# Infini-attention with a token MLP on one core: which of two query blocks comes first in the third logits step

## The chip, the cores and the metric

The kernel runs on one core of one Trainium2 chip. The metric is the device time of one execution in microseconds. Before the change the median was 721.3 us over three runs, from 720.23 to 722.08.

## The reference, cut to what matters

```python
# x: 2048 tokens x 1024; 32 heads of 32; 4 segments of 512 tokens
for s in range(4):
    logits = einsum('bhqd,bhkd->bhqk', qs, ks) * scale + causal_mask   # 512 x 512 per head
    p      = softmax(logits)
    a_dot  = einsum('bhqk,bhkd->bhqd', p, vs)
    a_mem  = (phi(qs) @ M) / (phi(qs) @ z)        # memory of the earlier segments
    o      = g * a_mem + (1 - g) * a_dot
    M, z   = M + phi(ks)^T vs, z + sum(phi(ks))
out = x + o @ wo + MLP_over_tokens(layernorm(x))   # 2048 -> 3584 -> 2048
```

The mask is causal. Of a 512-query segment, the key block `kb` (128 keys) is only needed by the queries from `128*kb` on. So the four key blocks need 512, 384, 256 and 128 queries. "The 256-query block" is key block 2, "the 128-query block" is key block 3.

## The kernel before

The attention is cut into 32 units, each one segment times four heads. The matrix engine (PE) gets one stream of matmuls per unit: three logits steps, four weighting steps (probabilities times values), the projections for later units, and between them pieces of the MLP and of the output projection ("main") that give the other engines time. The four heads of a unit sit on four groups of 32 rows of the array, so a logits step issues its matmuls as sets of four that run side by side ("row-tiled", "tiled" for short); matmuls on all 128 rows are called "full". The kernel has PE write its results to the banks of a memory called PSUM; VectorE or ScalarE copies a bank out (an "eviction") before the kernel lets PE write it again.

```python
PT_OFF = [0, 512, 896, 1152]        # where each key block lies in the probability tile pT
LOGIT_STEPS = [[0], [1], [2, 3]]    # the third step does two key blocks

def logits(self, u, step):
    kbs = self.LOGIT_STEPS[step]
    total = sum(SEG_L - P * kb for kb in kbs)
    with fw.group(reads=[R_kT[k], R_qT[k]], writes=R_bank[0:4]):
        col = 0
        for kb in kbs:
            n_q = SEG_L - P * kb
            for r in range(4):      # four row groups, four PSUM banks
                fw.mm(ps[:, r, col:col + n_q], kT[k][32*r:32*r+32, kb*P:(kb+1)*P],
                      qT[k][32*r:32*r+32, kb*P:SEG_L], start=True, stop=True, tile_position=(32*r, 0))
            col += n_q
    off = PT_OFF[kbs[0]]            # one exponential for the whole step (ScalarE)
    fw.op("act", activation(pT[:, :, off:off + total], ps[:, 0:4, 0:total], Exp, scale=SCALE), ...)
    for kb in kbs:                  # one diagonal mask per key block (GpSimd)
        d = pT[:, :, PT_OFF[kb]:PT_OFF[kb] + P]
        fw.op("pool", affine_select(d, d, ...), reads=[R_pTu[kb]], writes=[R_pTd[kb]])

def weigh(self, u, qb):             # query block qb needs the masked key blocks 0..qb
    reads = [R_pTu[kb] for kb in range(qb + 1)] + [R_pTd[kb] for kb in range(qb + 1)] + ...
    # ... matmuls into bank 4 + qb % 2, then a VectorE eviction of that bank

for u in range(N_UNIT):             # 32 units
    # ... logits 0, main_emit(n0), logits 1, main_emit(n1)
    self.logits(u, 2)
    # ... (two DMA transposes are issued)
    self.main_emit(n2)
    self.weigh(u, 0)
    self.weigh(u, 1)
    un = u + self.LEAD              # LEAD = 2
    if un < N_UNIT:
        self.proj_q(un, 0)          # query projection of a later unit: none for u = 30, 31
    self.weigh(u, 2)                # "third weighting step": needs the mask of key block 2
    m = u // 4 + 1
    if m < 2 * N_SEG:
        self.proj_v(m, u % 4, 2)    # none for u >= 28
    self.weigh(u, 3)                # "fourth weighting step": needs the mask of key block 3
    if un < N_UNIT:
        self.proj_k(un, 1)
    self.main_emit(n3)
```

The softmax here doesn't subtract the row's maximum and nothing guards it: scores larger than these inputs give would overflow.

Of the kernel before, what the change touches and what calls it, by code (L numbers as in the profile page):

```python
# [27 lines left out]
N_UNIT = N_SEG * N_GRP  # L28
VW = D_HEAD + 1
GW = 4 * VW  # L30
PT_OFF = [0, 512, 896, 1152]
PT_COLS = 1280


# [309 lines left out]
class _Kernel:  # L344
# [421 lines left out]
        self.fw.dma(self.pk[j][:], self.mtmp[1][:], reads=[self.R_mtmp[1]], writes=[self.R_pk[j]], transpose=True)  # L766


    LOGIT_STEPS = [[0], [1], [2, 3]]

    def logits(self, u, step):
        fw = self.fw
        k = u % 3
        kbs = self.LOGIT_STEPS[step]
        total = sum(SEG_L - P * kb for kb in kbs)
        with fw.group(reads=[self.R_kT[k], self.R_qT[k]], writes=self.R_bank[0:4]):
            col = 0
            for kb in kbs:
# [5 lines left out]
                col += n_q  # L784
        off = PT_OFF[kbs[0]]
        fw.op("act", lambda e: e.activation(self.pT[:, :, off:off + total], self.ps[:, 0:4, 0:total],  # L786
# [3 lines left out]
        for kb in kbs:  # L790
            d = self.pT[:, :, PT_OFF[kb]:PT_OFF[kb] + P]
            fw.op("pool", lambda e: e.affine_select(d, d, pattern=[[0, 4], [1, P]], compare_op=ALU.is_ge,  # L792
# [3 lines left out]
    def weigh(self, u, qb):  # L796
# [14 lines left out]
        with fw.group(reads=reads, writes=[self.R_bank[b]]):  # L811
            for r in range(4):
                for kb in range(qb + 1):
                    col = PT_OFF[kb] + (qb - kb) * P
                    fw.mm(self.ps[:, b, VW * r:VW * r + VW], self.pT[:, r, col:col + P], vA[:, kb, hl + r, :],
# [233 lines left out]
```

## Time and profile before

| what | before |
|---|---|
| median of the runs | 721.3 us |
| PE busy | 701.0 us (97%) |
| ScalarE, VectorE, GpSimd busy | 38%, 37%, 15% |
| PE's share of the chain that ended last | 93% |
| one unit of attention in the third segment | 15.6 us |

The page of the profile of the kernel before, parts 1 and 4 (busy time of each engine; the chain of work that ended last, by engine):

```profile
span 720.2 us, 11218 instructions
PE 701.0 (97%) x4818; PEld 324.6 (45%) x4818; DVE 263.1 (37%) x577; ACT 276.7 (38%) x314; POOL 111.1 (15%) x151
...
PE 93%; DVE 3%; ACT 2%; DMA 1%; issue 1%; SPq 0%; POOL 0%; DVEq 0%; ACTq 0%
```

PE bounds the kernel. A change can only matter if it lengthens PE's own stream or makes PE wait. The timeline of one ordinary unit (unit 13) shows the third step. The columns are: start in us, duration in us, engine, line, operation, output and inputs, shape, how many were merged, and in brackets the idle time just before with what ended it. PEld is the weight load of PE. Here and in the later timelines only the lines that the text reads are shown; lines between them are left out, also where no dots stand.

```profile
421.92 0.34 PE L192 MATMUL ps_all<-qT_1568,kT_1571 32*128 32x256 bf16 x8
422.19 1.90 PE L192 MATMUL ps_all<-gT,w2h_912 128*128 128x512 bf16 x8
422.31 1.45 ACT L786 ACTIVATE pT<-ps_all 128x1536 bf16<-128x1536 f32 x1 [0.66 <-PE ps_all L192]
423.83 1.23 POOL L792 TENSOR_SCALAR_AFFINE_SELECT pT<-pT 128x512 bf16<-128x512 bf16 x2 [1.47 <-ACT pT L786]
...
425.86 0.57 PEld L192 LDWEIGHTS ps_all<-vA_65,pT 128*128 128x128 bf16 x12
```

The eight row-tiled matmuls are merged into one line that shows the form of the first of them (256 columns). ScalarE then takes 1.45 us for the exponential, and GpSimd masks the two blocks in 1.23 us. The third weighting step (the 12 weight loads at 425.86) starts 0.80 us after both masks are done. There is no idle time in front of it.

The last two units are different, because nothing lies between the second and the third weighting step. The same view around unit 30; the first and the last line are the first logits weight loads of units 30 and 31:

```profile
677.89 0.10 PEld L192 LDWEIGHTS ps_all<-qT_1567,kT_1570 32*128 32x128 bf16 x4 [0.42 <-issue]
...
684.50 1.23 POOL L792 TENSOR_SCALAR_AFFINE_SELECT pT<-pT 128x512 bf16<-128x512 bf16 x2 [1.47 <-ACT pT L786]
...
684.96 0.77 DVE L826 CAST ost_1579<-ps_all 128x264 bf16<-128x264 f32 x2 [3.46 <-PE ps_all L192]
684.96 0.22 PE L192 MATMUL ps_all<-MZbf,pqT_1573 128*128 128x132 bf16 x1
...
685.54 0.45 PE L192 MATMUL ps_all<-vA_65,pT 128*128 128x33 bf16 x12 [0.36 <-DVE ost_1579 L826]
...
688.61 0.10 PEld L192 LDWEIGHTS ps_all<-qT_1568,kT_1571 32*128 32x128 bf16 x4 [0.42 <-issue]
```

Here PE waits in front of the third weighting step, for VectorE to empty the bank. At that moment the first mask (done after 0.64 us, at 685.14) is ready, the second one (done at 685.73) is not. The "pitch" of unit 30, from its first logits weight load to that of unit 31, is 10.72 us.

### The profile page before, as it was taken

Reading aid. Unit: us, or ns where it says so; the run is one execution under the profiler, and the core shown is the slowest. Engines: PE = TensorE matmul, PEld = TensorE weight load, DVE = VectorE, ACT = ScalarE, POOL = GpSimd, SP = SyncE. Lnnn points to the kernel's source line nnn. Section 1 sums busy time; section 2 is a strip of 40 time slices with the busy share of each in tenths; the row PEclk is TensorE's granted clock in tenths of the full one; section 3 lists DMA queues with packets and bytes.
Section 4 is the critical chain, followed back from the end, with each engine's and each line's share of the span. In section 5 each row is a group of like instructions: output and inputs, shape, how many; then the busy total and the mean of one; then the engine's idle time right before and its main releaser. Section 6 shows DMA issues by size and latency. Waiting matters only on the chain.

```text
span 720.2 us, 11218 instructions
## 1 busy us (share of the span) xinstructions
PE 701.0 (97%) x4818; PEld 324.6 (45%) x4818; DVE 263.1 (37%) x577; ACT 276.7 (38%) x314; POOL 111.1 (15%) x151
## 2 busy tenths in 40 slices
PE   6899999999999999999999999999999999999996
PEld 2344444444444444444444444444444444444442
DVE  4970000000002343344444545544555544344452
ACT  4551122111225445445444444443444444434420
POOL 1540000000001112211221111222111122111220
PEclk9999999999999999999999999999999999999999
DMA  9549677246016373872654625355352635527103
GB/s 269 142 115 177 144 190 192 64 112 124 12 60 163 66 125 87 127 118 63 123 117 87 126 44 126 75 109 120 79 125 45 126 86 97 111 53 117 30 27 114
DMA packets 211515, 77.17 MB, mean 107 GB/s; under 512 B 172554, under 2 KB 203274, under 8 KB 211466
## 3 DMA queue, kind: packets, MB, share of 16 engines
q1 hardware_dynamic: 211248, 76.43, 48.9%
q8 instruction: 38, 0.62, 0.4%
q14 instruction: 11, 0.09, 0.0%
q10 hardware_dynamic: 218, 0.02, 0.0%
HBM read 59.79 MB, written 5.24 MB: 90 GB/s over the span
## 4 chain that ended last, share of the span: by engine, by line
PE 93%; DVE 3%; ACT 2%; DMA 1%; issue 1%; SPq 0%; POOL 0%; DVEq 0%; ACTq 0%
PE ps_all L192 93%; DMA xin<-in_A_x_dram 1%; ACT etmp_1584 L749 1%; DVE kT_1570 L746 0%; DVE ln_st L606 0%; DVE kT_1572 L746 0%; DVE kT_1571 L746 0%; DVE ln_st L605 0%; ACT pT L786 0%; SPq L214 0%; DVE h L647 0%; ACT L749 0%; POOL h L651 0%; DVE fin_7771 L1016 0%; DVE fin_7770 L1016 0%
## 5 line engine op out<-in xcount | busy, mean ns | idle before, releaser
L786 ACT ACTIVATE pT<-ps_all 128x1536 bf16<-128x1536 f32 (+1 forms) x96 | 153.0, 1593 | 96.8 <-PE ps_all L192 96.8
L792 POOL TENSOR_SCALAR_AFFINE_SELECT pT<-pT 128x512 bf16<-128x512 bf16 x128 | 90.9, 723 | 561.5 <-ACT pT L786 561.5
L708 ACT ACTIVATE gT<-ps_all,b1c 128x512 bf16<-128x512 f32 x56 | 37.7, 689 | 134.5 <-PE ps_all L192 134.5
L192 PE MATMUL ps_all<-h,w1s_78 128*128 128x512 bf16 x320 | 73.9, 385 | 7.1 <-POOL h L651 3.5
L192 PE MATMUL ps_all<-h,w1s_79 128*128 128x512 bf16 x320 | 73.8, 385 | 0.0
L746 DVE CAST kT_1570<-ps_all 128x512 bf16<-128x512 f32 x11 | 7.6, 690 | 178.9 <-PE ps_all L192 178.9
L192 PE MATMUL ps_all<-gT,w2h_912 128*128 128x512 bf16 x224 | 56.3, 380 | 0.0
L192 PE MATMUL ps_all<-gT,w2h_914 128*128 128x512 bf16 x224 | 56.3, 380 | 0.0
L192 PE MATMUL ps_all<-h,w1s_80 128*128 128x512 bf16 x256 | 55.9, 379 | 0.0
L192 PE MATMUL ps_all<-gT,w2h_913 128*128 128x512 bf16 x224 | 53.9, 381 | 0.0
L192 PE MATMUL ps_all<-gT,w2h_911 128*128 128x512 bf16 x224 | 53.9, 381 | 0.0
L192 PEld LDWEIGHTS ps_all<-h,w1s_78 128*128 128x128 bf16 x320 | 31.4, 99 | 46.3 <-issue 8.5
L192 PEld LDWEIGHTS ps_all<-h,w1s_79 128*128 128x128 bf16 x320 | 31.7, 99 | 39.0 <-issue 2.3
L826 DVE CAST ost_1579<-ps_all 128x264 bf16<-128x264 f32 (+1 forms) x64 | 23.8, 394 | 69.2 <-PE ps_all L192 69.0
L826 DVE CAST ost_1580<-ps_all 128x264 bf16<-128x264 f32 (+1 forms) x64 | 23.8, 394 | 69.0 <-PE ps_all L192 68.9
L192 PEld LDWEIGHTS ps_all<-h,w1s_80 128*128 128x128 bf16 x256 | 25.0, 98 | 30.2
L749 ACT ACTIVATE etmp_1584<-ps_all 128x512 bf16<-128x512 f32 x24 | 14.3, 597 | 58.1 <-DVE kT_1572 L746 20.7
L192 PEld LDWEIGHTS ps_all<-gT,w2h_912 128*128 128x128 bf16 x224 | 20.6, 98 | 25.2 <-issue 2.5
L192 PEld LDWEIGHTS ps_all<-gT,w2h_914 128*128 128x128 bf16 x224 | 20.5, 98 | 24.7 <-issue 2.5
L192 PEld LDWEIGHTS ps_all<-gT,w2h_911 128*128 128x128 bf16 x224 | 19.3, 98 | 25.3 <-issue 6.4
L192 PEld LDWEIGHTS ps_all<-gT,w2h_913 128*128 128x128 bf16 x224 | 19.3, 98 | 25.3 <-issue 6.4
L192 PE MATMUL ps_all<-wo_sb,oT_1587 128*128 128x512 bf16 x128 | 30.2, 379 | 0.0
(154 smaller groups left out, 815.3 us busy)
## 6 DMA issues: line engine op xcount, KB each, us to landing
w1s_80<-in_B_w_dram SPq DMA_DIRECT2D x4, 1024.0 KB, 5.9
w1s_78<-in_B_w_dram SPq DMA_DIRECT2D x4, 1024.0 KB, 5.6
w1s_79<-in_B_w_dram SPq DMA_DIRECT2D x4, 1024.0 KB, 5.7
wq_907<-in_A_wq_dram SPq DMA_DIRECT2D x16, 256.0 KB, 3.5
wq_908<-in_A_wq_dram SPq DMA_DIRECT2D x16, 256.0 KB, 3.6
wk_909<-in_A_wk_dram SPq DMA_DIRECT2D x16, 256.0 KB, 3.8
wk_910<-in_A_wk_dram SPq DMA_DIRECT2D x16, 256.0 KB, 4.0
w2h_911<-in_B_w_dram SPq DMA_DIRECT2D x8, 448.0 KB, 4.8
```

Of the source, the lines that this page charges most:

```text
L192: ins = self.nc.tensor.matmul(*args, **kwargs)
L708: fw.op("act", lambda e: e.activation(self.gT[:, fc, half * 512:(half + 1) * 512], self.bank(b), ACT.Gelu_apprx_tanh, bias=self.b1c[:, fc: ...
L746: fw.op("dve", lambda e: e.tensor_copy(self.kT[k][:], self.bank(b)), reads=[self.R_bank[b]], writes=[self.R_kT[k]])
L749: fw.op("act", lambda e: e.activation(self.etmp[1][:], self.bank(b), ACT.Exp), reads=[self.R_bank[b]], writes=[self.R_etmp[1]])
L786: fw.op("act", lambda e: e.activation(self.pT[:, :, off:off + total], self.ps[:, 0:4, 0:total], ACT.Exp, scale=SCALE), reads=self.R_bank[0:4],
L792: fw.op("pool", lambda e: e.affine_select(d, d, pattern=[[0, 4], [1, P]], compare_op=ALU.is_ge, fill=0.0, base=0, channel_multiplier=-1), ...
L826: fw.op("dve", lambda e: e.tensor_copy(dst, self.ps[:, b, 0:n * VW]), reads=[self.R_bank[b]], writes=[self.R_ost[o][qb]])
```

## The change

The two key blocks of the third step trade places, both on PE and, because the same list drives the masks, on GpSimd. The offsets in the probability tile follow.

```diff
-PT_OFF = [0, 512, 896, 1152]
+PT_OFF = [0, 512, 1024, 896]
...
-    LOGIT_STEPS = [[0], [1], [2, 3]]
+    LOGIT_STEPS = [[0], [1], [3, 2]]
```

No matmul, byte, bank or engine is added or removed. One thing goes that the diff does not show: PE waited for GpSimd in the third and again in the fourth weighting step; now the third waits for the later mask, and the fourth needs no wait of its own.

## The prediction

> **What bounds the kernel now.** The matmul engine. The page gives PE 97% busy (701.0 of 720.2 us), and the chain of work that ended last lies 93% on PE. ScalarE (38%), VectorE (37%) and GpSimd (15%) have room. From 340 us on, units of attention follow each other every 15.6 us, and the timeline shows PE without a visible pause in them. So the change can only matter (a) through PE's own stream around the third logits step, or (b) where something it delays makes PE wait.
>
> **What it does.** Per unit (32 units) the same eight row-tiled matmuls run, four of 128 columns ahead of four of 256 instead of after them. The exponential keeps its shape, 128x1536 (1.45 us). The two diagonal masks on GpSimd swap: the 128-query block first, the 256-query block second. One PE wait for GpSimd goes (fourth weighting step), because the third now already waits for the later mask. No bytes, banks or engines change.
>
> **(a) PE's stream.** Start-to-start times of single matmuls in the trace, before: last full 512-column matmul to the first tiled one 312 ns (216 between full ones); 3-4 ns inside a set of four; 256-set to 128-set 109-110 ns; last 128-column one to the next full one 146-147 ns. Together about 589 ns. In the other steps the way out takes 264 ns after 384 columns and 316-317 after 512: columns/2.4 plus about 104; after 128 it is plus 93. After the change: 312 in, 56 between the sets (the Trainium skill, "TensorE: Matmul & The Clock Gate", Back-to-back issue gap: N/2.4 + 2.5 ns; the 216 and 110 measured here agree), 107 plus 93 to 104 out. Estimate 588 to 599 ns: nearly zero-sum, 0 to +10 ns a unit, 0 to +0.3 us in all. The skill's "TensorEngine Tiling (Array Packing)", Key Properties, says that changing the tiling mode drains the array; the 312 ns agrees, and the number of mode changes stays.
>
> **(b) Waits.** The third weighting step needs the 256-query mask. Before, that mask ends 0.95 us (units 0-7) or 1.39 us (8-29) ahead of that step's first weight load; as the second mask (637 ns long, starting 588 ns later) it still has 0.36 or 0.80 us, because a projection lies between. Only units 30 and 31 have none: the step's weight load starts at 685.51 and 696.23, the second mask ends at 685.73 and 696.45. With about 0.1 us from mask end to load (as seen after the VectorE eviction there) each loses about 0.3 us, on the chain: +0.6 us. The removed wait (51 ns in PE's queue) is hidden already.
>
> **Predicted: 722.0 us against 721.3 (+0.7), 8-in-10 range 720.5 to 723.6.** Most of the range is run-to-run scatter (720.2 to 722.1 before). Chances: faster by over 2% 0.005, within 2% 0.985, slower by over 2% 0.01.
>
> **What would show each step right or wrong.** In the timeline, third step 590-600 ns, with 56 between sets and 200-211 out. In units 30 and 31 a PE idle stretch ahead of the third weighting step growing from 0.36 to about 0.65 us, released by GpSimd; none in other units. Unit pitch 15.6 us and busy times unchanged.
>
> **What would make it wrong.** If weight loads of the second set cannot hide under 128 columns (90-94 ns each in the trace), the gap would be about 100 ns instead of 56: +1.4 us in all. If the way out of a 256-column set cost more than the other steps suggest, the same order. If GpSimd jitter used up the slack in units 0-7, up to a few tenths each. None reaches 2% (14 us).

## The result, and the profile after

The changed kernel ran in 721.11 us (median of four runs, 720.73 to 722.66), with 721.57 us for the kernel before over four runs (720.23 to 722.08). The ratio is 1.0001 with a 95% interval of 0.998 to 1.0021: the same. Ratios here are the mean time of one kernel's runs over that of the other's of the same rounds, so they are not quite the ratio of the medians. The kernels of one submission also share their runs of the kernel before, which explains the slightly different medians for it below.

The page of the changed kernel, the same lines:

```profile
span 720.9 us, 11097 instructions
PE 695.0 (96%) x4728; PEld 324.6 (45%) x4818; DVE 263.1 (36%) x577; ACT 276.8 (38%) x314; POOL 111.4 (15%) x151
...
PE 92%; DVE 3%; ACT 2%; issue 1%; DMA 1%; SPq 0%; POOL 0%; DVEq 0%; ACTq 0%
```

PE's busy time seems to fall by 6 us. It did not: the trace has 4728 matmul records for 4818 weight loads, so 90 matmul records are missing. The weight loads, of which none is missing, have the same 324.6 us, and if the same 90 matmuls are left out of the trace before, its busy time falls to 695.1 us too. (The other 31 of the 121 instructions that the page counts fewer are the waits that went.) Unit 13 in the timeline after:

```profile
422.05 0.34 PE L192 MATMUL ps_all<-qT_1568,kT_1571 32*128 32x128 bf16 x8
422.33 1.90 PE L192 MATMUL ps_all<-gT,w2h_912 128*128 128x512 bf16 x8
422.44 1.45 ACT L786 ACTIVATE pT<-ps_all 128x1536 bf16<-128x1536 f32 x1 [0.66 <-PE ps_all L192]
423.96 1.23 POOL L792 TENSOR_SCALAR_AFFINE_SELECT pT<-pT 128x512 bf16<-128x512 bf16 x2 [1.47 <-ACT pT L786]
...
426.00 0.56 PEld L192 LDWEIGHTS ps_all<-vA_65,pT 128*128 128x128 bf16 x12
```

The first form is now 128 columns. Everything else keeps its distance: from the logits matmuls to the exponential 0.39 us in both, to the third weighting step 3.94 and 3.95 us. The merged lines hide single matmuls, so the table gives the median time from start to start of single records in both traces, over the 32 units (the first row is called the way in, the fifth the way out; in units 0 to 7 the way in is 318 to 320 ns in both):

| third step | before | after |
|---|---|---|
| last full matmul to first tiled one | 312 ns | 312 ns |
| across the first set of four | 10 ns | 10 ns |
| last of the first set to first of the second | 110 ns | 56 ns |
| across the second set | 11 ns | 11 ns |
| last tiled one to the next full one | 147 ns | 200 ns |
| sum of the step, median where no record is missing | 588 ns | 589 ns |

Unit 30 in the timeline after:

```profile
678.02 0.10 PEld L192 LDWEIGHTS ps_all<-qT_1567,kT_1570 32*128 32x128 bf16 x4 [0.42 <-issue]
...
684.64 1.23 POOL L792 TENSOR_SCALAR_AFFINE_SELECT pT<-pT 128x512 bf16<-128x512 bf16 x2 [1.47 <-ACT pT L786]
...
685.10 0.77 DVE L826 CAST ost_1579<-ps_all 128x264 bf16<-128x264 f32 x2 [3.46 <-PE ps_all L192]
685.10 0.22 PE L192 MATMUL ps_all<-MZbf,pqT_1573 128*128 128x132 bf16 x1
...
685.96 0.45 PE L192 MATMUL ps_all<-vA_65,pT 128*128 128x33 bf16 x12 [0.65 <-DVE ost_1579 L826]
...
689.03 0.10 PEld L192 LDWEIGHTS ps_all<-qT_1568,kT_1571 32*128 32x128 bf16 x4 [0.42 <-issue]
```

The idle time ahead of the third weighting step grew from 0.36 to 0.65 us, and the pitch of unit 30 from 10.72 to 11.01 us. The trace can be cut into four stretches, each measured between the first logits weight loads of two units:

| stretch | before | after | difference |
|---|---|---|---|
| start to unit 0 | 225.147 us | 225.274 us | +0.127 |
| units 0 to 29 | 452.739 us | 452.747 us | +0.008 |
| unit 30 | 10.722 us | 11.009 us | +0.287 |
| unit 31 to the end | 31.621 us | 31.907 us | +0.286 |

The change costs 0.58 us behind the first logits, all but 0.008 us of it in the last two units. That is 0.08% of the time and lies under the scatter of whole runs. Part of that scatter can be seen: in the eleven traces the first stretch, which none of the edits touches, takes anything from 223.25 to 225.59 us, while the stretches behind it repeat to within about 0.01 us where the code is alike.

One line must not be taken at its word: the profile says that VectorE (`DVE ost_1579`) ended the idle time of 0.65 us. The two merged evictions ended at 685.87 us, and so did the two masks (start plus duration in the lines above), so the merged lines cannot tell the two apart. Single records can. Narrower windows of the same trace show the first of the two evictions and the first weight load of the step alone:

```profile
685.10 0.43 DVE L826 CAST ost_1579<-ps_all 128x264 bf16<-128x264 f32 x1 [3.46 <-PE ps_all L192]
...
685.93 0.10 PEld L192 LDWEIGHTS ps_all<-vA_65,pT 128*128 128x128 bf16 x1 [0.76 <-issue]
```

The step writes the bank that this first eviction empties; the second belongs to the other bank. In the kernel before, the weight load started 0.115 us after the end of the first eviction. After the change it starts 0.405 us after it, but only 0.07 us after the end of the later mask. So by time it is the mask; the experiments test it.

### The profile page after: what moved, and what is told of

The parts are those of the page before. It is cut to its first block, busy times and chain, and to the rows that moved or that the text cites. A ratio compares the mean times of both kernels' runs of the same rounds, so it can differ in the third digit from the quotient of the medians.

```text
span 720.9 us, 11097 instructions
## 1 busy us (share of the span) xinstructions
PE 695.0 (96%) x4728; PEld 324.6 (45%) x4818; DVE 263.1 (36%) x577; ACT 276.8 (38%) x314; POOL 111.4 (15%) x151
## 4 chain that ended last, share of the span: by engine, by line
PE 92%; DVE 3%; ACT 2%; issue 1%; DMA 1%; SPq 0%; POOL 0%; DVEq 0%; ACTq 0%
PE ps_all L192 92%; DMA xin<-in_A_x_dram 1%; ACT etmp_1584 L749 1%; DVE kT_1570 L746 0%; DVE ln_st L606 0%; DVE kT_1572 L746 0%; DVE kT_1571 L746 0%; DVE ln_st L605 0%; ACT pT L786 0%; SPq L214 0%; DVE h L647 0%; ACT L749 0%; DVE ost_1579 L826 0%; POOL h L651 0%; DVE fin_7739 L1016 0%
## 5 line engine op out<-in xcount | busy, mean ns | idle before, releaser
L192 PE MATMUL ps_all<-gT,w2h_914 128*128 128x512 bf16 x211 | 55.0, 380 | 1.0 <-issue 0.5
L192 PE MATMUL ps_all<-gT,w2h_912 128*128 128x512 bf16 x211 | 54.4, 379 | 1.4 <-issue 1.1
L192 PE MATMUL ps_all<-gT,w2h_913 128*128 128x512 bf16 x220 | 53.7, 381 | 0.2
L192 PE MATMUL ps_all<-gT,w2h_911 128*128 128x512 bf16 x221 | 53.6, 380 | 0.3 <-issue 0.2
```

What stands on the lines that cost most here:

```text
L192: ins = self.nc.tensor.matmul(*args, **kwargs)
```

## The experiments

The theory: the order on PE is free, and the whole cost is the mask order, which moves the mask that the third weighting step needs 0.59 us later; that costs time only where nothing covers it (units 30 and 31). The rivals: the matmul order itself costs something (weight loads that do not hide, a longer way out), or the added wait belongs to VectorE, as the profile names it.

### One half of the change at a time

The kernel before with only the masks swapped:

```diff
-        for kb in kbs:
+        for kb in reversed(kbs):
             d = self.pT[:, :, PT_OFF[kb]:PT_OFF[kb] + P]
```

> The kernel before, with the two masks of the third step swapped on GpSimd (128-query mask first) and the matmul order left alone. Theory (the mask order is the whole effect): the third step's matmuls keep 312 / 110 / 147 ns and 589 ns in all; units 0 to 29 keep their pitch; the start-to-start time from unit 30's to unit 31's first logits weight load grows from 10.72 to about 11.01 us, and the time from unit 31's to the end grows by the same 0.29 us; PE's idle time ahead of the third weighting step of these two units is 0.65 us instead of 0.36. Rival (the order of the matmuls on PE or the different exponential layout causes the delay): 10.72 us, as before.

The changed kernel with only the masks swapped back (the same edit on the changed kernel):

> The changed kernel, with the mask order put back (256-query mask first). Theory: the third step's matmuls show 312 / 56 / 200 ns, again 589 ns in all, and unit 30's pitch is 10.72 us as before: nothing is left of the change in the time. Rival: unit 30's pitch stays at 11.01 us, or all units change.

One look each: 720.64 and 721.30 us, which tells nothing at this size; the traces do. The third weighting step of unit 30 in the timeline of the masks-only kernel (buffer numbers are left out of the names in these traces):

```profile
683.94 0.45 PE L192 MATMUL ps_all<-vA,pT 128*128 128x33 bf16 x12 [0.65 <-DVE ost L826]
```

And of the matmuls-only kernel:

```profile
684.88 0.45 PE L192 MATMUL ps_all<-vA,pT 128*128 128x33 bf16 x12 [0.36 <-DVE ost L826]
```

| | before | after | masks only | matmuls only |
|---|---|---|---|---|
| gap between the sets, and way out | 110, 147 ns | 56, 200 ns | 110, 147 ns | 56, 200 ns |
| units 0 to 29 | 452.739 | 452.747 | 452.747 | 452.743 us |
| unit 30 | 10.722 | 11.009 | 11.010 | 10.723 us |
| unit 31 to the end | 31.621 | 31.907 | 31.907 | 31.623 us |

The masks alone reproduce the whole difference, and the matmul order alone leaves nothing. The added 0.29 us are also not VectorE's: in units 30 and 31 the weight load starts 0.115 us after the first eviction where the masks have their old order, and 0.40 us after it where they are swapped. (The 0.36 us of PE idle time that stood there before the change are VectorE's.) The removed wait of the fourth weighting step goes with the mask order too: 127 semaphore waits with the masks alone, 158 with the matmuls alone. The two were not separated.

### Nothing to cover the mask, in every unit

To lift the effect above the scatter, the projection that covers the mask is moved behind the third weighting step, once in each kernel:

```diff
             self.weigh(u, 1)
+            self.weigh(u, 2)
             un = u + self.LEAD
             if un < N_UNIT:
                 self.proj_q(un, 0)
-            self.weigh(u, 2)
```

> The kernel before with the query projection moved behind the third weighting step in every unit, so that nothing covers the 256-query mask (128-query block still last). Theory: PE now waits for the first mask or the VectorE eviction in every unit: about 0.6 us in units 0 to 7 and 0.36 us in the others, in all about +13 us against the kernel before (about 734 us).

> The same move in the changed kernel. Theory: each unit waits for the second mask, 0.55 to 0.59 us longer in units 0 to 7 and 0.29 us longer in units 8 to 31 than the same move in the kernel before: +11 us against that kernel (about 745 us). Rival (mask order has no bearing on the time): the same time as that kernel within noise.

With the 128-query block last (order of before) the time is 737.78 us (four runs, ratio to the kernel before 1.0225, interval 1.0202 to 1.0247). With it first it is 750.25 us (four runs, ratio 1.0404, 1.0388 to 1.0419). The same swap that could not be seen in the time now costs 12.5 us between the medians. In the traces the difference is 4.68 us in units 0 to 7 (0.58 each), 6.23 us in units 8 to 29 (0.28 each) and 0.56 us from unit 30 on, together 11.5 us where 11 had been expected; the rest of the 12.5 us is within the scatter of whole runs (736.43 to 738.80 us for the first of the two).

Unit 1 in the timeline with the order of before:

```profile
247.37 0.50 DVE L826 CAST ost<-ps_all 128x132 bf16<-128x132 f32 x2 [3.49 <-PE ps_all L192]
247.41 1.22 POOL L792 TENSOR_SCALAR_AFFINE_SELECT pT<-pT 128x512 bf16<-128x512 bf16 x2 [1.27 <-ACT pT L786]
...
248.14 0.46 PE L192 MATMUL ps_all<-vA,pT 128*128 128x33 bf16 x12 [0.61 <-POOL pT L792]
```

And with the order of the change:

```profile
248.20 0.50 DVE L826 CAST ost<-ps_all 128x132 bf16<-128x132 f32 x2 [3.49 <-PE ps_all L192]
248.24 1.22 POOL L792 TENSOR_SCALAR_AFFINE_SELECT pT<-pT 128x512 bf16<-128x512 bf16 x2 [1.27 <-ACT pT L786]
...
249.56 0.46 PE L192 MATMUL ps_all<-vA,pT 128*128 128x33 bf16 x12 [1.19 <-POOL pT L792]
```

In these early units the evictions are short (0.50 us) and done long before, and the profile itself names GpSimd. The idle time grows by 0.58 us, the distance of the two masks. In the changed order the weight load of this step starts 70 ns after the end of the second mask in every unit, and the same 70 ns stand in units 30 and 31 of the changed kernel. So there too the mask was the last to come, and the name of VectorE in the bracket was wrong.

The sum of the first of the two expectations was too small: +13 us was expected, and the medians differ by 16.9. The mis-sized term is above all units 8 to 29; units 0 to 7 lost 0.66 us each, where 0.6 had been expected. The idle time in the bracket is 0.36 us there, as expected, but each unit lost 0.52 us. In start-to-start times it is plain: the last matmul before the wait and the first one behind it lie 576 ns apart, where 57 ns is the pace without a wait. The bracket counts from the modelled end of the last matmul (record of 0.22 us), most of which lies in the shadow of the next matmul when there is one. The Trainium skill, "Perfetto Trace Analysis", Tensor Engine Instruction, says that the reported end of a PE instruction is computed and not observed. No run here shows where the true end lies, but the start-to-start times do not need it: they put 0.16 us between the bracket and the loss (0.52 less 0.36).

### What a further row-tiled set costs

The prediction had used two different sizes for the way out (columns/2.4 plus 104 ns after one set, plus 93 ns after two) without a reason. In the kernel before, the second step's 384 columns were cut into three sets:

```diff
-                for r in range(4):
-                    fw.mm(ps[:, r, col:col + n_q], ..., qT[..., kb * P:SEG_L], ...)
+                wid = P if kb == 1 else n_q
+                for c0 in range(0, n_q, wid):
+                    for r in range(4):
+                        fw.mm(ps[:, r, col + c0:col + c0 + wid], ..., qT[..., kb * P + c0:kb * P + c0 + wid], ...)
```

> The kernel before with the second step's four 384-column matmuls cut into three sets of four 128-column ones (same weights, same results). It asks what one more row-tiled set costs PE. Reading A (a set starts N/2.4 + 2.5 ns after the LAST matmul of the set before): gaps between sets of 56 and 56 ns, and about 147 ns out. Reading B (each row group runs on its own, and only the first set starts some 10 ns later than its record): 56 and then about 46 ns. The whole step takes 586 ns uncut; A gives 312 + 10 + 56 + 10 + 56 + 10 + 147 = 601 ns, B 591 ns.

Measured: gaps of 56 and 45 ns, a way out of 147 ns, and 591 ns for the step, against 586 uncut. That is what reading B expected: each row group goes on by itself, and the first set really starts about 10 ns later than its record says. The true start is in no record, so this is the reading that fits and not a thing seen. It would explain the 93 and 104 ns as one number seen from two starts. It would also say why the order was free: the sum of the step depends on the columns and on the number of sets, not on their order. Cutting one set in three cost 5 ns.

### Giving the last two units cover

In the changed kernel, eight "main" matmuls of units 30 and 31 (in each of the two, two of the MLP and six of the output projection) were moved to where the other units have the projection:

```diff
             if un < N_UNIT:
                 self.proj_q(un, 0)
+            else:
+                self.main_emit(8)
+                n3 -= 8
             self.weigh(u, 2)
```

> The changed kernel, with 8 of the MLP matmuls of units 30 and 31 moved from behind the fourth weighting step to between the second and the third, where the projection lies in the other units (8 x 216 ns = 1.7 us of cover). Theory: the PE idle time of 0.65 us in each of the two units goes; unit 30's pitch is about 10.36 us instead of 11.01, and the whole 1.3 us shorter than the changed kernel, 0.7 us shorter than the kernel before (about 720.5 us; hardly clear of the scatter of whole runs, so the pitch is what counts). Rival (the wait would come back later, at another resource): pitch between 10.4 and 11.0.

The time is 719.61 us (five runs, ratio 0.9986, interval 0.9974 to 0.9999). Around unit 30 in its timeline:

```profile
683.19 0.22 PE L192 MATMUL ps_all<-MZbf,pqT 128*128 128x132 bf16 x1
683.25 0.59 PE L192 MATMUL ps_all<-gT,w2h 128*128 128x512 bf16 x2
683.67 1.46 PE L192 MATMUL ps_all<-wo_sb,oT 128*128 128x512 bf16 x6
684.97 0.46 PE L192 MATMUL ps_all<-vA,pT 128*128 128x33 bf16 x12
```

No idle time is left. Unit 30's pitch is 10.20 us, 0.81 us less than in the changed kernel where 0.65 had been expected: the same 0.16 us per wait as above, now from the other side. The part behind the first logits is 1.62 us shorter than in the changed kernel and 1.04 us shorter than in the kernel before. So the wait did not come back elsewhere. The whole-run interval only just leaves out 1, so the pitch carries this.

### A larger wait in the first segment

In the kernel before, the chain of work that ended last leaves PE at one more place that repeats. Ahead of the first logits step of units 1 to 8 it runs over VectorE and ScalarE, because the first logits step needs bank 1, and the key projection had written it just before. Unit 2 in the timeline of the kernel before:

```profile
252.94 0.69 DVE L746 CAST kT_1570<-ps_all 128x512 bf16<-128x512 f32 x1 [0.90 <-PE ps_all L192]
...
253.73 0.60 ACT L749 ACTIVATE etmp_1584<-ps_all 128x512 bf16<-128x512 f32 x1 [2.55 <-DVE kT_1570 L746]
...
254.47 0.40 PE L192 MATMUL ps_all<-qT_1569,kT_1572 32*128 32x512 bf16 x4 [0.27 <-ACT etmp_1584 L749]
```

The copy and then the exponential have to leave the bank, one after the other; the six MLP matmuls behind the projection are not enough for that. The value projection needs only one copy. So the two trade places:

```diff
-            m = u // 4 + 1
-            if m < 2 * N_SEG:
-                self.proj_v(m, u % 4, 2)
-            self.weigh(u, 3)
             if un < N_UNIT:
                 self.proj_k(un, 1)
+            self.weigh(u, 3)
+            m = u // 4 + 1
+            if m < 2 * N_SEG:
+                self.proj_v(m, u % 4, 2)
```

> The kernel before, with the key projection moved ahead of the fourth weighting step and the value projection behind it. In units 1 to 8 PE waits 0.34 us for bank 1 (VectorE copy, then the exponential for the keys) ahead of the first logits step: 649 instead of 312 ns from the last full matmul to the first tiled one. Theory: the value projection's bank is freed by one ScalarE copy of 0.60 us under the same six matmuls, so the wait goes: 8 x 0.34 = 2.7 us shorter, about 718.7 us. Rival: PE then only arrives earlier at the exponential of step 1 and waits there instead (0 us gained).

The time is 717.92 us (five runs, ratio 0.9966, interval 0.9953 to 0.998). Unit 2 in its timeline:

```profile
250.61 1.46 PE L192 MATMUL ps_all<-gT,w2h 128*128 128x512 bf16 x6
250.81 0.60 ACT L760 ACTIVATE vA<-ps_all 128x512 bf16<-128x512 f32 x1 [0.98 <-PE ps_all L192]
...
252.00 0.40 PE L192 MATMUL ps_all<-qT,kT 32*128 32x512 bf16 x4
```

ScalarE's copy is done at 251.41 us, 0.6 us ahead of the logits, and PE's idle time is gone. Units 0 to 7 became 2.66 us shorter together, 2.7 us had been expected.

Both edits on the kernel before:

> The kernel before with both the cover in units 30 and 31 and the key projection ahead of the value projection. Theory: the two gains add up, 0.7 + 2.7 = 3.4 us, about 718 us, faster than both kernels; in it the order of the two blocks would not matter any more.

716.68 us (five runs, 716.22 to 717.74), ratio 0.9946, interval 0.9933 to 0.9958. The part behind the first logits is 3.73 us shorter than in the kernel before. The two gains (2.66 us, and 2 x 0.52 us for the two waits of the order of before) add up. The expectation had 3.4 us, because it priced the two waits by the bracket (0.36 us each).

And the same with the change on top:

> The fastest kernel so far (cover in units 30 and 31, key projection ahead of the value projection), with the 128-query block put first again. Theory: with cover in every unit the order is free: the stretch from the first logits weight load to the end is 491.35 us as in that kernel, to within 0.05 us, unit 30's pitch 10.20 us, and the time about 716.7 us. Rival (the order costs time by another path as well): unit 30's pitch or the last stretch 0.1 to 0.3 us longer.

717.45 us (six runs, 716.42 to 718.28), ratio 0.9949, interval 0.9933 to 0.9965. Behind the first logits it takes 491.361 us against 491.353, and unit 30 takes 10.202 us in both. With cover in every unit the order of the two blocks is free; the medians of the two, 0.8 us apart, lie inside each other's scatter. Both versions beat the kernel before by about half a per cent: the intervals leave out 1. Against the changed kernel they were not timed side by side; the stretch behind the first logits is 4.3 us shorter than its 495.66 us.

## Why the prediction was right

- The bound: PE, as read. The result did not contradict it.
- PE's stream: "588 to 599 ns" was predicted and 588 to 589 measured; the gap of 56 ns was exact, and the way out of 200 ns lies at the lower end of 200 to 211. Units 0 to 29 together changed by 0.008 us, where 0 to 0.3 had been allowed. The lower end fits the 10 ns of the first set, as the three-set run reads.
- The Trainium skill's gap, as the prediction took it from "TensorE: Matmul & The Clock Gate", Back-to-back issue gap (N/2.4 + 2.5 ns), agrees here with 216 ns for 512 columns and 56 ns for 128.
- The waits: 0.3 us in each of units 30 and 31 was predicted, and 0.287 and 0.286 measured. The weight load came 70 ns after the mask, where 0.1 us had been assumed. The idle time grew from 0.36 to 0.65 us as predicted. "None in other units" held, with slacks of 0.36 us (units 0 to 7) and 0.80 us (units 8 to 29) left.
- "Released by GpSimd" is true by the experiments, but the profile's bracket says VectorE. As a sign to look for in the profile it was wrong.
- "Busy times unchanged" was wrong as a sign for PE, because matmul records were missing; the busy time of the weight loads shows it.
- The total: +0.7 us was predicted, +0.58 us is in the trace behind the first logits, and the medians (721.11 against 721.57 us) cannot resolve it. The run times fit a forecast of no change just as well, so they are no evidence for the mechanism; the traces and the two kernels without cover are.

## What to carry to other kernels

A reorder that keeps the count and the sizes of PE's work can be free on PE, as here (588 against 589 ns a step); look then for what else the same list orders, here two masks on another engine, and for the one consumer that needs the moved result. A delay costs nothing where the slack is larger, so look for the units at the edge of a loop in which the covering work is missing. To price a wait of PE, take the start-to-start time less the usual pace, not the idle time in the bracket. When an effect lies under the scatter, cut the trace at markers that both kernels have, and take the cover away in every unit to lift it above the scatter.

## What the Trainium skill lacked or had wrong

- "TensorE: Matmul & The Clock Gate", Back-to-back issue gap, gives about 131 ns per matmul as the sustained pace of pairs of weight load and matmul at N = 512, and calls N/2.4 + 2.5 ns the isolated gap. Behind the first logits, 1572 of the 1669 steps from one full matmul of 512 columns to the next take 214 to 216 ns and the others 225 to 227, so the formula is the sustained pace here.
- The same page, The mechanism, under "What overlaps and what doesn't", says that a weight load overlaps with matmuls in flight only where the row group differs. Here the record of the next weight load on all 128 rows mostly starts 1 to 2 ns after a full matmul starts, and the pairs still keep 216 ns. The same section names a background weight buffer as a second case, which would fit; no run here tests it.
- "TensorEngine Tiling (Array Packing)", Key Properties, says that a change of the tiling mode drains the array, without a figure. Here the way in costs 96 ns (312 less 216 ns), and the way out takes columns/2.4 plus 93 ns in the two-set steps, plus 104 ns in the one-set steps. That the drain is what costs this is not shown.
- No page was found that says what a further set in the same mode costs: in the three-set run two more sets made the step 5 ns longer (586 to 591 ns), with gaps of 56 and 45 ns.
- "Perfetto Trace Analysis", Tensor Engine Instruction, calls PE's end times modelled, but does not say how far idle times counted from them fall short of the time lost: a wait shown as 0.36 us cost 0.52 us, one shown as 0.65 us cost 0.81 us.
